# A cross network of six layers: x0 read in four-row runs, every x0 transpose on TensorE, the program order fixed

## The chip, the cores and the metric

The kernel runs on one core of a Trainium2 chip. The metric is the device time of one execution, in microseconds. The kernel before takes 142.92 us (median of three runs, 142.19 to 143.85).

## The reference

The input `x0` is a 4096 x 416 matrix in bfloat16, with six weight matrices of 416 x 416 and six bias rows of 416. Each layer multiplies the current `x` by a matrix, adds a bias row, multiplies the result element by element with `x0` and adds the old `x`:

```python
def reference(x0, ws, bs):
    x = x0
    for l in range(ws.shape[0]):
        x = x0 * (x @ ws[l] + bs[l]) + x
    return x
```

The rows of the batch never mix, so the kernel is free to choose which row lies in which place, if input and output agree.

## The kernel before, in words

The first five layers work on the transposed matrix: features on the 128 partitions, batch rows along the free dimension. The 416 features are three full blocks of 128 (`m` or `k` = 0, 1, 2; tile `XM`) and a remainder of 32 (tile `XR`, which stacks four column groups of 32 partitions each). The 4096 rows are two slabs of 2048 (`s` = 0, 1), and a slab is four groups `g` of 512 columns.

One **unit** is one layer on one slab; there are ten, and the first of them also prepares the data. On TensorE a unit runs 12 matmuls of 512 columns for `m` = 0 (three `k` for each group, line 167), four small matmuls with the remainder's weights (line 172) that finish block 0, four that open block 1, then 12 and 12 for blocks 1 and 2, the four that finish block 2, and the remainder's own product `pr` (lines 178 and 183). ScalarE then adds the bias while it moves each pair of groups out of PSUM into a tile `t` (line 154; line 160 for the remainder), and VectorE multiplies by `x0` and adds the old `x` (lines 155 and 156; 161 and 162).

The last layer works the other way around: rows on the partitions, features along the free dimension, so that its result can be written out as it is. Eight **quads** of four 128-row blocks each take 12 matmuls (line 258), four with the remainder (264) and four with the bias row (267). ScalarE copies out of PSUM (282), VectorE multiplies by `X0rows` (283) and adds the x of the layer before (284 for the 384 full features, 285 for the 32 of the remainder), and SyncE's queue (SP) starts the write (286). For this the x of the fifth layer has to be turned back: DMA transposes on SP write its three full blocks into `XLrows` (line 190) and its remainder into `scrR` (line 242). The last quad is handled in four single blocks (lines 289 to 293).

At the start, `x0` arrives in chunks of four 128-row blocks (`X0rows`, lines 81 to 85, with layer 0's weights behind the first chunk). TensorE transposes slab 0's chunks into PSUM, 12 transposes a chunk (line 125), and VectorE (127) and ScalarE (129) copy them to `XM[0]`; 16 small transposes make the remainder (136, 138). Slab 1 comes by another way: its blocks 0 and 1 through two DMA transposes straight from `x0` (line 96), its block 2 and remainder from a tile `slab1` by TensorE (lines 144, 136), in the middle of unit 0. Its plain rows, which only the last layer reads, are loaded later (102, 103).

All PSUM tiles come from one pool of four slots of 4 KB a partition. A pair of result tiles takes two slots; a group of transposes, `pr` or `tpr` takes one. A slot is free again when its reader has finished.

The order in which each engine runs its instructions is set, in the kernel before, by the framework's planner, which starts from the program's order and may move an instruction ahead of another one that is not ready by its reckoning. Each engine then works strictly in that order. SP takes its DMA issues in turn, and each carries one of eight semaphores, so an issue also waits until the eighth DMA before it has landed.

Of the kernel before, what the change touches and what calls it, by code (L numbers as in the profile page):

```python
# [16 lines left out]
def kernel(  # L17
# [27 lines left out]
    x0_v = x0.rearrange("(bt p) d -> p bt d", p=P)  # L45
    out_v = out.rearrange("(bt p) d -> p bt d", p=P)
# [13 lines left out]
    XLrows = big.tile([P, NBT, NK * P], BF16)  # L60
    scrR = [big.tile([P, 4, P], BF16, name=f"scrR{s}") for s in range(NS)]
    slab1 = big.tile([P, 16, 160], BF16)
# [13 lines left out]
    pe_filler(7)  # L76
# [4 lines left out]
    nc.sync.dma_start(X0rows[:, 0:4, :], x0_v[:, 0:4, :])  # L81
    load_wm(0)
    nc.sync.dma_start(X0rows[:, 4:8, :], x0_v[:, 4:8, :])
    nc.sync.dma_start(X0rows[:, 8:12, :], x0_v[:, 8:12, :])
    nc.sync.dma_start(X0rows[:, 12:16, :], x0_v[:, 12:16, :])
# [4 lines left out]
    with nc.allow_non_contiguous_dma(reason="tiny corner blocks"):  # L90
        for g in range(NG):
            nc.gpsimd.dma_start(WD[32 * g:32 * g + 32, :, g, :], ws[:, NK * P:D, NK * P:D].rearrange("l r n -> r l n"))  # L92
# [9 lines left out]
    nc.sync.dma_start(X0rows[:, 16:24, :], x0_v[:, 16:24, :])  # L102
    nc.sync.dma_start(X0rows[:, 24:32, :], x0_v[:, 24:32, :])
    for g in range(NG):
        nc.gpsimd.dma_start(bLr[32 * g:32 * g + 1, :], bs[LL:LL + 1, :])

# [12 lines left out]
    def x0_transposes_main(g):  # L119
        tp = psum.tile([P, NK, CW], BF16, tag="ps", name="tp")  # L120
        c0 = col0(0, g)
        for k in range(NK):
            for i in range(4):
                bt = 4 * g + i
                nc.tensor.transpose(tp[:, k, 128 * i:128 * i + 128], X0rows[:, bt, 128 * k:128 * k + 128], ident[:])  # L125
            if k < 2:
                nc.vector.tensor_copy(XM[0][:, k, c0:c0 + CW], tp[:, k, :])  # L127
            else:
                nc.scalar.copy(XM[0][:, k, c0:c0 + CW], tp[:, k, :])  # L129

    def x0_transposes_rem(s):
        tpr = psum.tile([P, CW], BF16, tag="ps", name="tpr")
        for i in range(4):
            for g in range(NG):
                src = X0rows[:, 4 * g + i, NK * P:D] if s == 0 else slab1[:, 4 * g + i, P:P + R]
                nc.tensor.transpose(tpr[32 * g:32 * g + 32, 128 * i:128 * i + 128], src, ident[:],
                                    tile_position=(0, 32 * g))
        nc.scalar.copy(XR[0][:, CW * s:CW * s + CW], tpr[:])

    def x0_transposes_k2_s1():  # L140
        for h in range(2):
            tk = psum.tile([P, 2 * CW], BF16, tag="ps", name="tk")
            for j in range(8):
                nc.tensor.transpose(tk[:, 128 * j:128 * j + 128], slab1[:, 8 * h + j, 0:P], ident[:])  # L144
            c0 = SW + 2 * CW * h
            if h == 0:
                nc.vector.tensor_copy(XM[0][:, 2, c0:c0 + 2 * CW], tk[:])
            else:
                nc.scalar.copy(XM[0][:, 2, c0:c0 + 2 * CW], tk[:])  # L149
# [14 lines left out]
    def mm_full(l, s, m, g, pts, cur, first, last):  # L164
        c0 = col0(s, g)
        for k in range(NK):
            nc.tensor.matmul(pts[g // 2][:, g % 2, :], lhsT=WM[:, l, k, 128 * m:128 * m + 128], rhs=cur[:, k, c0:c0 + CW],  # L167
                             start=(first and k == 0), stop=(last and k == NK - 1))
# [25 lines left out]
    for l in range(LL):  # L194
        nxt, nxtR = XM[1 + (l % 2)], XR[1 + (l % 2)]
        feeds_last = (l == LL - 1)
        for s in range(NS):
# [3 lines left out]
            if first_unit:  # L201
                x0_transposes_main(0)
                bias_setup()
                x0_transposes_main(1)
                mm_full(l, s, 0, 0, pts0, cur, True, False)
                x0_transposes_main(2)
                mm_full(l, s, 0, 1, pts0, cur, True, False)
                x0_transposes_main(3)
                mm_full(l, s, 0, 2, pts0, cur, True, False)
                x0_transposes_rem(0)  # L210
                mm_full(l, s, 0, 3, pts0, cur, True, False)
            else:
                for g in range(NG):
                    mm_full(l, s, 0, g, pts0, cur, True, False)
# [16 lines left out]
            if first_unit:  # L231
                x0_transposes_k2_s1()
                x0_transposes_rem(1)
            mm_row(l, s, 2, pts2, curR, False, True)
            pr = psum.tile([P, CW], FP32, tag="ps", name="pr")
            mm_rem(l, s, pr, cur, curR)
            for h in range(2):
                ew_main(l, s, 2, h, pts2[h], cur, nxt)
            ew_rem(l, s, pr, curR, nxtR)
            if feeds_last:  # L240
                xl_dmat(s, 2, nxt)
                nc.sync.dma_start_transpose(out=scrR[s][:], in_=nxtR[:, CW * s:CW * s + CW])
# [27 lines left out]
    def ew_q(q, py):  # L270
        s, i = quads[q]
        last_quad = (q == NQ - 1)
        for h in range(2):
            bts = [16 * s + 4 * (2 * h + gl) + i for gl in range(2)]
# [3 lines left out]
            x0v = X0rows[:, bts[0]:bts[1] + 1:4, :]  # L278
            xlv = XLrows[:, bts[0]:bts[1] + 1:4, :]
            xrv = scrR[s][:, i, 64 * h:64 * h + 64].rearrange("p (a r) -> p a r", a=2)  # L280
            if not last_quad:
                nc.scalar.copy(tv, py[h][:, :, 0:D])  # L282
                nc.vector.tensor_tensor(out=tv, in0=tv, in1=x0v, op=ALU.mult)  # L283
                nc.vector.tensor_tensor(out=o[:, :, 0:KD], in0=tv[:, :, 0:KD], in1=xlv, op=ALU.add)  # L284
                nc.vector.tensor_tensor(out=o[:, :, KD:D], in0=tv[:, :, KD:D], in1=xrv, op=ALU.add)
                nc.sync.dma_start(out_v[:, bts[0]:bts[1] + 1:4, :], o[:])
            else:
                for gl in range(2):
                    nc.scalar.copy(tv[:, gl, :], py[h][:, gl, 0:D])
                    nc.vector.tensor_tensor(out=tv[:, gl, :], in0=tv[:, gl, :], in1=X0rows[:, bts[gl], :], op=ALU.mult)  # L290
                    nc.vector.tensor_tensor(out=o[:, gl, 0:KD], in0=tv[:, gl, 0:KD], in1=XLrows[:, bts[gl], :], op=ALU.add)
                    nc.vector.tensor_tensor(out=o[:, gl, KD:D], in0=tv[:, gl, KD:D], in1=xrv[:, gl, :], op=ALU.add)
                    nc.sync.dma_start(out_v[:, bts[gl], :], o[:, gl, :])
# [40 lines left out]
```

## Time and profile before

| | |
|---|---|
| median of three runs | 142.92 us (142.19 to 143.85) |
| profiled execution, span from first to last instruction | 141.9 us |
| TensorE busy | 130.0 us, 92% of the span |
| VectorE busy | 109.3 us, 77% |
| ScalarE busy | 87.0 us, 61% |
| GpSimd busy | 8.4 us, 6% |
| chain that ended last | TensorE 71%, VectorE 11%, DMA 9%, ScalarE 3% |
| HBM read, written | 6.68 MB, 3.41 MB |

The profile is that of one execution. Its span runs from the first instruction to the last; the run's time also holds what lies around the span. Three stages have to be read apart: the start until unit 1 of ten begins on TensorE (about 26 us), the nine further units (to about 115 us), and the last layer with its writes.

### The profile page before, as it was taken

To read this page: it belongs to the slowest core of one execution; us is meant where nothing else is said; L and a number is where in the kernel's file an instruction comes from. 1 tells how busy PE (TensorE), PEld (TensorE's weight loads), DVE (VectorE), ACT (ScalarE), POOL (GpSimd) and SP (SyncE) were. 2 spreads that over 40 slices of the span, in tenths; PEclk is the share of its full clock that TensorE was granted. 3 is DMA by queue.
4 is the path that set the end of the run, shared out by engine and by line. 5 is a ranking of instruction groups with operands and counts; after the bars stand their busy time and mean duration, and the time that the engine had idled before them with its cause. 6 is when DMAs were issued, how large, how long until landed. Compare 5 with 4: busy or idle time off the path is not lost.

```text
span 141.9 us, 2405 instructions
## 1 busy us (share of the span) xinstructions
PE 130.0 (92%) x910; PEld 56.0 (39%) x910; DVE 109.3 (77%) x207; ACT 87.0 (61%) x97; POOL 8.4 (6%) x21
## 2 busy tenths in 40 slices
PE   5759998999999999999999999999999999999910
PEld 2426345434343343343333433433433345445400
DVE  1214178769878888898798799787987989999891
ACT  4011593875695695677657956956776578548530
POOL 8950000000000000000000000000000000000000
PEclk9968999999999999999999999999999999999995
DMA  4999999980000000000000000000089999965542
GB/s 136 294 280 130 232 249 273 330 251 10 0 2 0 0 7 0 0 0 0 0 5 0 0 0 0 5 0 0 0 166 173 146 200 187 229 226 178 175 162 92
DMA packets 31899, 14.69 MB, mean 104 GB/s; under 512 B 20618, under 2 KB 31888, under 8 KB 31888
## 3 DMA queue, kind: packets, MB, share of 16 engines
q1 hardware_dynamic: 31472, 14.38, 43.1%
q0 software_dynamic: 416, 0.16, 0.5%
q8 instruction: 7, 0.11, 0.3%
q14 instruction: 4, 0.03, 0.1%
HBM read 6.68 MB, written 3.41 MB: 71 GB/s over the span
## 4 chain that ended last, share of the span: by engine, by line
PE 71%; DVE 11%; DMA 9%; ACT 3%; issue 2%; SPq 1%; DVEq 0%
DMA X0rows<-in_x_dram 6%; PE pr L183 5%; DMA out_dram<-o 3%; PE pr L178 2%; DVE t L283 2%; DVE XM_87 L156 2%; DVE t L155 2%; DVE o L284 2%; ACT XM_86 L129 1%; PE pt_1184 L167 1%; PE pt_1166 L167 1%; PE pt_1081 L167 1%; PE pt_982 L167 1%; PE pt_784 L167 1%; PE pt_388 L167 1%
## 5 line engine op out<-in xcount | busy, mean ns | idle before, releaser
L167 PEld LDWEIGHTS <-WM 128*128 128x128 bf16 x360 | 33.7, 98 | 45.4 <-issue 8.6
L155 DVE TENSOR_TENSOR t<-t,XM_86 128x1024 bf16<-128x1024 bf16 x60 | 41.2, 686 | 13.5 <-ACT t L154 12.9
L156 DVE TENSOR_TENSOR XM_87<-t,XM_88 128x1024 bf16<-128x1024 bf16 x24 | 16.6, 690 | 2.1
L156 DVE TENSOR_TENSOR XM_88<-t,XM_87 128x1024 bf16<-128x1024 bf16 x24 | 16.6, 691 | 1.4
L258 PEld LDWEIGHTS <-XM_87 128*128 128x128 bf16 x96 | 9.0, 98 | 8.5 <-issue 1.8
L127 DVE COPY XM_86<-tp 128x512 bf16<-128x512 bf16 x8 | 3.3, 422 | 9.3 <-PE tp L125 9.3
L129 ACT COPY XM_86<-tp 128x512 bf16<-128x512 bf16 x4 | 2.3, 585 | 11.6 <-PE tp L125 11.6
L283 DVE TENSOR_TENSOR t<-t,X0rows 128x832 bf16<-128x832 bf16 x14 | 8.2, 586 | 0.9 <-ACT t L282 0.8
L156 DVE TENSOR_TENSOR XM_87<-t,XM_86 128x1024 bf16<-128x1024 bf16 x12 | 8.3, 690 | 0.3
L284 DVE TENSOR_TENSOR o<-t,XLrows 128x768 bf16<-128x768 bf16 x14 | 7.8, 557 | 0.5
L125 PE MATMUL tp<-ident,X0rows 128*128 128x128 bf16 x48 | 5.2, 250 | 2.9 <-DMA X0rows<-in_x_dram 1.7
L160 ACT ACTIVATE t<-pr,bR 128x512 bf16<-128x512 f32 x10 | 6.9, 689 | 0.0
L125 PEld LDWEIGHTS <-X0rows 128*128 128x128 bf16 x48 | 3.9, 114 | 5.5 <-DMA X0rows<-in_x_dram 2.8
L172 PEld LDWEIGHTS <-WR 32*128 32x128 bf16 x120 | 2.4, 91 | 8.4 <-issue 8.1
L74 PE MATMUL wps<-warm 128*128 128x512 bf16 x7 | 3.2, 630 | 1.5 <-DVE dz L67 1.5
L161 DVE TENSOR_TENSOR t<-t,XR_89 128x512 bf16<-128x512 bf16 x10 | 4.2, 418 | 0.0
L183 PEld LDWEIGHTS <-WM 128*32 128x32 bf16 x120 | 3.2, 97 | 2.2
L183 PE MATMUL pr<-XM_88,WM 128*32 128x512 bf16 x48 | 3.3, 379 | 0.0
L183 PE MATMUL pr<-XM_87,WM 128*32 128x512 bf16 x48 | 3.3, 379 | 0.0
L167 PE MATMUL pt_141<-XM_86,WM 128*128 128x512 bf16 x6 | 2.8, 544 | 0.1
L149 ACT COPY XM_86<-tk 128x1024 bf16<-128x1024 bf16 x1 | 1.0, 1012 | 2.3 <-PE tk L144 2.3
L92 POOL DMA_DIRECT2D WD<-in_ws_dram x4 | 2.3, 573 | 0.9 <-DMA WR<-in_ws_dram 0.9
(288 smaller groups left out, 255.4 us busy)
## 6 DMA issues: line engine op xcount, KB each, us to landing
out_dram<-o SPq DMA_DIRECT2D x14, 208.0 KB, 2.2
WM<-in_ws_dram SPq DMA_DIRECT2D x6, 312.0 KB, 6.0
X0rows<-in_x_dram SPq DMA_DIRECT2D x4, 416.0 KB, 7.5
X0rows<-in_x_dram SPq DMA_DIRECT2D x2, 832.0 KB, 8.8
slab_85<-in_x_dram SPq DMA_DIRECT2D x1, 640.0 KB, 10.9
WR<-in_ws_dram SPq DMA_DIRECT2D x4, 130.0 KB, 6.4
out_dram<-o SPq DMA_DIRECT2D x4, 104.0 KB, 1.7
WR<-in_ws_dram POOLq DMA_DIRECT2D x4, 26.0 KB, 5.7
```

What stands on the lines that cost most here:

```text
L125: nc.tensor.transpose(tp[:, k, 128 * i:128 * i + 128], X0rows[:, bt, 128 * k:128 * k + 128], ident[:])
L127: nc.vector.tensor_copy(XM[0][:, k, c0:c0 + CW], tp[:, k, :])
L129: nc.scalar.copy(XM[0][:, k, c0:c0 + CW], tp[:, k, :])
L155: nc.vector.tensor_tensor(out=t[:], in0=t[:], in1=XM[0][:, m, c0:c0 + 2 * CW], op=ALU.mult)
L156: nc.vector.tensor_tensor(out=nxt[:, m, c0:c0 + 2 * CW], in0=t[:], in1=cur[:, m, c0:c0 + 2 * CW], op=ALU.add)
L160: nc.scalar.activation(tr[:, 0:CW], pr[:], ACT.Identity, bias=bR[:, l:l + 1], scale=1.0)
L161: nc.vector.tensor_tensor(out=tr[:, 0:CW], in0=tr[:, 0:CW], in1=XR[0][:, CW * s:CW * s + CW], op=ALU.mult)
L167: nc.tensor.matmul(pts[g // 2][:, g % 2, :], lhsT=WM[:, l, k, 128 * m:128 * m + 128], rhs=cur[:, k, c0:c0 + CW], start=(first and k == 0), ...
L183: nc.tensor.matmul(pr[32 * g:32 * g + 32, :], lhsT=WM[:, l, k, NK * P:D], rhs=cur[:, k, c0:c0 + CW], start=False, stop=(k == NK - 1), tile ...
L258: nc.tensor.matmul(py[g // 2][:, g % 2, 0:D], lhsT=cur[:, k, q_cols(q, g)], rhs=WM[:, l, k, :], start=((not rem_first) and k == 0), stop=( ...
L283: nc.vector.tensor_tensor(out=tv, in0=tv, in1=x0v, op=ALU.mult)
L284: nc.vector.tensor_tensor(out=o[:, :, 0:KD], in0=tv[:, :, 0:KD], in1=xlv, op=ALU.add)
```

## The change

- **Row order.** Chunk `c` now holds rows 512c to 512c+511 with row 512c + 4p + j in partition p, place j. A partition's share of a chunk is four neighbouring rows, one run of 3328 bytes in place of four of 832. The output uses the same order, in writes of one row per partition and block as before.
- **Loads.** Chunk 0 is loaded in two halves of two rows each. The four chunks of slab 1 follow chunk 3 at once and are the only load of those rows; the tile `slab1`, the two DMA transposes from `x0` and the two later loads are gone. `WD`, the remainder's corner weights, is no longer loaded by DMA but copied by GpSimd out of `WR`.
- **Transposes of slab 1.** All three blocks are made by TensorE in unit 0, 16 transposes each, half of each copied by VectorE and half by ScalarE. Blocks 0 and 1 stand where block 2 stood; block 2 and the remainder stand behind `pr`, and ahead of the bias additions for block 2 of unit 0.
- **Slab 0's chunks.** The 12 transposes run block by block; two of the three 512-column results leave in one VectorE copy of 1024 columns. Of the seven warm-up matmuls, two move behind chunk 0's transposes. The bias transposes move behind the first matmuls.
- **Order.** `tc.manual_schedule()` fixes each engine's order to that of the program; the planner no longer moves anything.
- **Last layer.** The remainder of the fifth layer's result goes by four DMA transposes a slab (32 partitions each) straight into the last 32 columns of `XLrows`, in place of one a slab into `scrR`. The two additions (lines 284 and 285) become one of 832 columns.

```diff
-    x0_v = x0.rearrange("(bt p) d -> p bt d", p=P)
-    out_v = out.rearrange("(bt p) d -> p bt d", p=P)
+    x0_v = x0.rearrange("(c p j) d -> p c j d", p=P, j=4)
+    out_v = out.rearrange("(c p j) d -> p c j d", p=P, j=4)
...
+    ctx.enter_context(tc.manual_schedule())
...
-    pe_filler(7)
+    pe_filler(5)
...
+    load_x0(0, 0, 2)
+    load_x0(0, 2, 4)
     load_wm(0)
+    for c in range(1, 4):
+        load_x0(c)
...
-    with nc.allow_non_contiguous_dma(reason="320B row segments"):
-        nc.sync.dma_start(slab1[:], x0_v[:, 16:32, 2 * P:D])
-    for k in range(2):
-        nc.sync.dma_start_transpose(out=XM[0][:, k, SW:2 * SW], in_=x0[SW:2 * SW, 128 * k:128 * k + 128])
+    for c in range(4, 8):
+        load_x0(c)
...
+    for g in range(NG):
+        nc.gpsimd.tensor_copy(WD[32 * g:32 * g + 32, 0, g, :], WR[32 * g:32 * g + 32, 0, NK * P:D])
...
     def x0_transposes_main(g):
+        tg = psum.tile([P, 4 * CW], BF16, tag="ps", name="tg")
+        for i in range(4):
+            for k in range(NK):
+                c = CW * k + 128 * i
+                nc.tensor.transpose(tg[:, c:c + 128], X0rows[:, 4 * g + i, 128 * k:128 * k + 128], ident[:])
+        nc.vector.tensor_copy(XM[0][:, 0:2, c0:c0 + CW], tg[:, 0:2 * CW].rearrange("p (k c) -> p k c", k=2))
+        nc.scalar.copy(XM[0][:, 2, c0:c0 + CW], tg[:, 2 * CW:3 * CW])
...
+    def x0_transposes_s1(k):
+        tk = psum.tile([P, 2, 2 * CW], BF16, tag="ps", name="tk")
         for h in range(2):
             for j in range(8):
+                nc.tensor.transpose(tk[:, h, 128 * j:128 * j + 128], X0rows[:, 16 + 8 * h + j, 128 * k:128 * k + 128], ident[:])
             c0 = SW + 2 * CW * h
             if h == 0:
+                nc.vector.tensor_copy(XM[0][:, k, c0:c0 + 2 * CW], tk[:, h, :])
             else:
+                nc.scalar.copy(XM[0][:, k, c0:c0 + 2 * CW], tk[:, h, :])
...
             if first_unit:
                 x0_transposes_main(0)
-                bias_setup()
+                pe_filler(2)
                 x0_transposes_main(1)
                 mm_full(l, s, 0, 0, pts0, cur, True, False)
+                bias_setup()
...
             if first_unit:
-                x0_transposes_k2_s1()
-                x0_transposes_rem(1)
+                x0_transposes_s1(0)
+                x0_transposes_s1(1)
             mm_row(l, s, 2, pts2, curR, False, True)
             pr = psum.tile([P, CW], FP32, tag="ps", name="pr")
             mm_rem(l, s, pr, cur, curR)
+            if first_unit:
+                x0_transposes_s1(2)
+                x0_transposes_rem(1)
             for h in range(2):
                 ew_main(l, s, 2, h, pts2[h], cur, nxt)
             ew_rem(l, s, pr, curR, nxtR)
             if feeds_last:
                 xl_dmat(s, 2, nxt)
-                nc.sync.dma_start_transpose(out=scrR[s][:], in_=nxtR[:, CW * s:CW * s + CW])
+                for g in range(NG):
+                    nc.sync.dma_start_transpose(out=XLrows[:, 16 * s + 4 * g:16 * s + 4 * g + 4, NK * P:D],
+                                                in_=nxtR[32 * g:32 * g + 32, CW * s:CW * s + CW])
...
-                nc.vector.tensor_tensor(out=o[:, :, 0:KD], in0=tv[:, :, 0:KD], in1=xlv, op=ALU.add)
-                nc.vector.tensor_tensor(out=o[:, :, KD:D], in0=tv[:, :, KD:D], in1=xrv, op=ALU.add)
+                nc.vector.tensor_tensor(out=o[:], in0=tv, in1=XLrows[:, bts[0]:bts[1] + 1:4, :], op=ALU.add)
```

More of the change, by code (lines that the diff above doesn't have):

```diff
@@ L59 @@
     X0rows = big.tile([P, NBT, D], BF16)
-    XLrows = big.tile([P, NBT, NK * P], BF16)
-    scrR = [big.tile([P, 4, P], BF16, name=f"scrR{s}") for s in range(NS)]
-    slab1 = big.tile([P, 16, 160], BF16)
+    XLrows = big.tile([P, NBT, D], BF16)
     XM = [big.tile([P, NK, B], BF16, name=f"XM{i}") for i in range(3)]
     XR = [big.tile([P, NS * CW], BF16, name=f"XR{i}") for i in range(3)]
+    ctx.enter_context(tc.manual_schedule())
     nc.vector.memset(warm[:], 0.5)
@@ L165, in mm_full @@
         c0 = col0(s, g)
-        for k in range(NK):
+        ks = (0, 1, 2)
+        for n, k in enumerate(ks):
             nc.tensor.matmul(pts[g // 2][:, g % 2, :], lhsT=WM[:, l, k, 128 * m:128 * m + 128], rhs=cur[:, k, c0:c0 + CW],
-                             start=(first and k == 0), stop=(last and k == NK - 1))
+                             start=(first and n == 0), stop=(last and n == NK - 1))
     def mm_row(l, s, m, pts, curR, first, last):
@@ L241 @@
                 xl_dmat(s, 2, nxt)
[L242 removed]
+                for g in range(NG):
+                    nc.sync.dma_start_transpose(out=XLrows[:, 16 * s + 4 * g:16 * s + 4 * g + 4, NK * P:D],
+                                                in_=nxtR[32 * g:32 * g + 32, CW * s:CW * s + CW])
         cur, curR = nxt, nxtR
@@ L273, in ew_q @@
         for h in range(2):
-            bts = [16 * s + 4 * (2 * h + gl) + i for gl in range(2)]
+            c = 4 * s + 2 * h
+            bts = [4 * c + i, 4 * c + 4 + i]
             t = tpool.tile([P, 2 * CW], BF16, name="t")
```

42 lines of the change are left out of this document (9 added, 33 removed).

## The prediction

> **What bounds the kernel now.** I read the page first, then busy time by stage, then the chain of waits, then the start in order of time.
>
> ```profile
> span 141.9 us, 2405 instructions
> ...
> PEclk9968999999999999999999999999999999999995
> ```
>
> The stages (start:end, length, busy time of PE, PEld, DVE, ACT and POOL, granted clock, DMA share, GB/s):
>
> ```profile
> 5.00:8.40 3.40, 1.09 (x16) 0.70 (x14) 1.09 (x4) 0.58 (x1) 2.51 (x5) 1.00 1.03 308
> 8.40:11.90 3.50, 3.03 (x16) 1.76 (x16) 1.10 (x3) 0.00 (x0) 1.55 (x4) 0.51 1.22 232
> 26.10:114.60 88.50, 88.50 (x581) 35.22 (x578) 76.31 (x126) 61.27 (x64) 0.00 (x0) 1.00 0.20 42
> 119.70:124.90 5.20, 5.20 (x43) 2.62 (x41) 4.82 (x13) 3.26 (x5) 0.00 (x0) 1.00 0.98 240
> ```
>
> From 26.1 to 114.6 PE never rests: nine units of 9.83 us. A pair of quads of the last layer is full of PE too (5.20 of 5.20). The change touches no matmul of these, and a fixed order can't pack a full PE any better, so it can act only before 26.1 and in the tail. The chain (start, length, work) gives the start:
>
> ```profile
> 2.31 0.51 SPq L84
> ...
> 2.86 9.17 DMA X0rows<-in_x_dram
> ...
> 16.83 0.39 PE pt_141 L172 x2
> ...
> 24.46 0.41 PE tpr L136 x16
> ...
> 25.19 0.33 PE pr L178 x4
> 25.52 0.65 PE pr L183 x12
> 26.16 1.40 PE pt_370 L167 x6
> 27.57 1.29 PE pt_371 L167 x6
> ...
> 114.63 1.16 PE pt_1269 L258 x6
> ```
>
> Chunk 3 of x0 lands at 12.03. At 17.26, which I call T0, ScalarE begins unit 0's bias additions. Unit 1's first matmul is at 26.16, T0 + 8.9. So the change is worth (new T0) + (new distance from T0 to unit 1) - 26.16, and what the tail gives.
>
> **From T0 to unit 1: longer.** Unit 0 now, in order of time:
>
> ```profile
> 17.26 1.11 ACT L154 ACTIVATE t<-pt_141,bM 128x1024 bf16<-128x1024 f32 x1 [0.48 <-PE pt_142 L172]
> ...
> 18.27 1.11 ACT L154 ACTIVATE t<-pt_142,bM 128x1024 bf16<-128x1024 f32 x1
> 18.41 0.69 DVE L155 TENSOR_TENSOR t<-t,XM_86 128x1024 bf16<-128x1024 bf16 x1 [3.43 <-ACT t L154]
> ...
> 22.57 1.06 PE L144 MATMUL tk<-ident,slab_85 128*128 128x128 bf16 x16
> ...
> 23.66 1.01 ACT L149 COPY XM_86<-tk 128x1024 bf16<-128x1024 bf16 x1 [2.27 <-PE tk L144]
> 23.73 0.68 DVE L147 COPY XM_86<-tk 128x1024 bf16<-128x1024 bf16 x1
> ...
> 25.58 0.59 ACT L138 COPY XR_89<-tpr 128x512 bf16<-128x512 bf16 x1
> ```
>
> I lay the new order on these prices, relative to T0. The first 16 transposes start as before at 22.57 - 17.26 = 5.31 and end at 6.37; block 1's end at 7.43. VectorE is busy with eight products and sums from 18.41 to 23.73 in both kernels, so its copies run 6.47 to 7.15 and to 7.83; ScalarE's run 6.40 to 7.41 and to 8.46. The four L172 matmuls (16.83 to 17.26: 0.43) end at 7.86, `pr` (0.33 + 0.65) at 8.84, block 2's transposes at 9.90. Now comes the new wait. The four PSUM slots hold the two result tiles of block 2, `pr` and block 2's transposes. The first three are read by bias additions that stand, in the fixed order, behind the copy of the remainder, so that remainder's slot can only be the transposes' own: it waits for ScalarE's half (9.92 + 1.01 = 10.93). Then 0.41 of transposes and a ScalarE copy of 0.59 end at 12.0, which frees the first slot for unit 1. Its second slot comes 1.11 later, before PE has done the 1.29 of the first pair. So unit 1 starts at T0 + 12.0, not + 8.9: 3.1 us lost, of which 2.12 are 32 transposes that DMA did before and most of the rest is PE waiting for slots. Unit 1's own bias additions come later than unit 0's last, so nothing further runs on.
>
> **T0: earlier.** The start, and two answers on DMA packets (from 1.5 to 9.15 us, then from 2.5 to 4.0):
>
> ```profile
> 4.10 0.10 PEld L125 LDWEIGHTS <-X0rows 128*128 128x128 bf16 x1 [0.38 <-DMA X0rows<-in_x_dram]
> ...
> 6.94 0.18 PE L115 MATMUL pb<-ident,bsb 6*32 6x6 bf16 x4
> ...
> 8.86 0.34 PEld L125 LDWEIGHTS <-X0rows 128*128 128x128 bf16 x4 [1.83 <-DMA X0rows<-in_x_dram]
> ```
>
> ```profile
> DMA packets 2970, 2.18 MB, mean 285 GB/s; under 512 B 557, under 2 KB 2970, under 8 KB 2970
> ```
>
> ```profile
> DMA packets 639, 0.52 MB, mean 346 GB/s; under 512 B 16, under 2 KB 639, under 8 KB 639
> ```
>
> By 9.15 us 2.18 MB had moved, more than the 2.02 MB of four chunks (0.426 each) and layer 0's weights (0.319). Yet chunk 1 was there only at 8.86 and chunk 3 at 12.03: 557 packets of the slab behind had passed already, so the chunks wait for the slowest of the 16 DMA engines. The late end for the new kernel is therefore as now: 8.86 and 12.03. The early end has no laggard and the 346 GB/s of the second row throughout: chunk 0 (1.23 us at that rate) was used at 4.10, an offset of 2.87; chunk 1 closes 1.17 MB, 2.87 + 3.38 = 6.25; chunk 3 closes 2.02 MB, 8.72. Long runs cut the packets of a chunk from 512 to 128 or 256, so a delay per packet shrinks; what makes an engine lag the trace doesn't say. I take the middle: 7.55 and 10.4. The extra issue ahead of chunk 3 (0.51 on SP) hides behind engines that are still moving chunk 0.
>
> Here the Trainium skill speaks against the change: "DMA: Bandwidth & Descriptors", Specifications, has 512 bytes as enough for line rate, and runs of 832 are above it. By it nothing lands sooner, which is the slow rival below; the laggard here can't be explained by it.
>
> Behind chunk 1 PE has three groups of 12 transposes (1.06 x 12/16 = 0.80 each), four of three matmuls (half of 1.29, 0.65 each), seven bias transposes (0.18 x 7/4 = 0.32), the remainder (0.41) and the L172 matmuls (0.43): 6.16 us; behind chunk 3, 0.80 + 0.65 + 0.41 + 0.65 + 0.43 = 2.94. The copies out of PSUM, one of 1024 columns for two of 512 among them, run beside the next matmuls. What happens to chunk 0 (two halves, five warm-up matmuls and two later) ends before chunk 1 is there and costs nothing; if chunk 1 came at once, it would be some 0.43 us (two of the 1.29 for six). T0 is the later of 7.55 + 6.16 = 13.7 and 10.4 + 2.94 = 13.3, at full clock: 13.7, against 17.26.
>
> Slab 1's four chunks are needed at T0 + 5.3 = 19.0. 1.70 MB at 285 GB/s behind 10.4 is 16.4: covered by 2.6 us. `WD` is needed by `pr` at T0 + 7.9 = 21.6; its source lands about 10:
>
> ```profile
> WR<-in_ws_dram POOLq DMA_DIRECT2D x4, 26.0 KB, 5.7
> ```
>
> No row prices GpSimd's copies, but 11 us of cover take them; at worst they would delay `pr` by what exceeds it.
>
> **The last layer: a little shorter.**
>
> ```profile
> 119.46 0.58 DVE L283 TENSOR_TENSOR t<-t,X0rows 128x832 bf16<-128x832 bf16 x1
> ...
> 120.08 0.56 DVE L284 TENSOR_TENSOR o<-t,XLrows 128x768 bf16<-128x768 bf16 x1
> ...
> 120.56 0.18 DVE L285 TENSOR_TENSOR o<-t,scrR_83 128x64 bf16<-128x64 bf16 x1
> 120.66 0.58 DVE L283 TENSOR_TENSOR t<-t,X0rows 128x832 bf16<-128x832 bf16 x1
> ...
> 129.15 0.56 DVE L284 TENSOR_TENSOR o<-t,XLrows 128x768 bf16<-128x768 bf16 x1
> ...
> 133.67 0.59 DVE L283 TENSOR_TENSOR t<-t,X0rows 128x832 bf16<-128x832 bf16 x1 [0.27 <-ACT t L282]
> ```
>
> Half a quad takes 0.62 + 0.48 + 0.10 = 1.20 on DVE; one addition of 832 columns takes 0.48 x 832/768 = 0.52 for 0.58, saving 0.06. That counts only where DVE is the bound, behind the last wait at 133.67: four halves, 0.24 us. Ahead of that it is slack.
>
> SP gets eight issues for two:
>
> ```profile
> 110.16 1.56 SPq L242 DMA_TRANSPOSE scrR_83<-XR_90  x1
> ...
> 120.15 1.39 SPq L242 DMA_TRANSPOSE scrR_84<-XR_90  x1
> 121.63 14.92 SPq L286 DMA_DIRECT2D out_dram<-o  x14
> ```
>
> ```profile
> L190 SPq DMA_TRANSPOSE XLrows<-XM_87 x6: 1698/1912/2964, 102.1 to 117.9; - x6
> ```
>
> ```profile
> scrR_83<-XR_90 SPq DMA_TRANSPOSE x1, 4.3
> scrR_84<-XR_90 SPq DMA_TRANSPOSE x1, 2.6
> ```
>
> Each new one moves a quarter: 0.35 to 1.56 on SP; I take 1.4, since L190 with four times the data takes only 1.9. In the times of before: four from 110.16 to 115.8, three L190 (held back by them) to 121.5, the last of slab 1's begins at 125.7 and lands 2.6 later at 128.3. DVE reads it at 129.15: 0.85 to spare. Writes start 5.4 us later, queued behind them on SP, and catch up: an issue about every half microsecond against a tile every 1.14.
>
> **Sum.** 13.7 + 12.0 - 26.16 - 0.24 = -0.7 against the span of 141.9. The median of 142.92 lies 1.0 above that span, and I keep that distance: 142.2.
>
> **Rivals.**
> - *No laggard.* Long runs take the lag away, chunk 1 at 6.25: T0 = 12.4, 2.0 us faster, 140.9. For it: packets of a chunk fall to a quarter. Against: no row ties the lag to packets. Chance 0.24.
> - *The join doesn't wait.* If the slots or the order don't work as I read them, the 1.03 behind 9.90 and the 0.7 until 12.0 go: 1.7 less, 140.5. Chance 0.08.
> - *Half clock.* From 8.40 PE ran at 0.51 after a stretch with 1.09 of 3.40 busy. If that returns in this window, 3.5 us of the work behind chunk 1 run at half speed: T0 = 15.4, +1.0, 143.9. New is an earlier chunk 1 and two fillers in the stretch, which make about 1.8 of 3.4 busy. Chance 0.13. The Trainium skill ("TensorE: Matmul & The Clock Gate", Part 1) has the clock halve after an idle window; by that rule it stays full, but the trace halved it behind a window that was a third busy.
> - *Nothing lands sooner (slower).* Chunk 1 at 8.86 makes T0 15.0, and with half clock until 11.9 (as now) 16.5: +2.1, 145.0. It decides from chunk 1 later than 8.2, where T0 passes 14.4 and the gain no longer pays the 3.1 at the join. For it: DMA is full already at 346 GB/s. Chance 0.15.
> - *SP's transposes bind.* At 1.56 each and 4.3 to land, the last is there at 131.1, 2.0 late; DVE's slack (5.20 - 4 x 1.14 = 0.6 a pair) leaves 1.4: 143.6. Chance 0.07.
>
> My forecast keeps 0.33; a fifth of it lies beyond 1% faster.
>
> **Numbers.** One per cent, 1.4 us, is what a measurement of this kernel can tell from no change. Faster: 0.24 + 0.08 + 0.07 = 0.39. Slower: 0.15, and 0.05 from the upper ends of half clock and SP: 0.20. Same: 0.41. The likeliest case alone spans 141.2 to 143.2; the range reaches to the fast rivals' side, 140.1, and into the slow one, 144.3.
>
> **What would show it.** Chunk 1's first use between 6.3 and 8.9; the ScalarE start near 13.7; the remainder's transposes idling for the ScalarE copy of block 2; unit 1 about 12 behind T0; units of 9.83; an addition of 832 columns at about 0.6; no DVE wait at the second slab's first quad. A distance T0 to unit 1 near 10, or unit 1 before 24, would make me wrong.

## The result and the profile after

The changed kernel is slower: 150.2 us (median of four, 149.18 to 150.96) against 143.38 for the kernel before beside it (142.19 to 144.44), a ratio of 1.052 (95% interval 1.045 to 1.059). The forecast was 142.2, with 144.3 as its upper end. Where a ratio stands beside a median in what follows, it leaves out disturbed executions, so the two need not divide out.

The profiled execution of the changed kernel is the 149.18. Its page begins:

```profile
span 147.4 us, 2458 instructions
...
PEclk9968999999999999999999999999999999999975
```

The span is 5.4 us longer than before's 141.9. The view by stages (start:end, length, busy time of PE, PEld, DVE, ACT and POOL, granted clock, DMA share, GB/s) says where it isn't:

```profile
5.35:8.76 3.41, 1.48 (x17) 0.88 (x15) 0.69 (x2) 0.59 (x1) 0.40 (x2) 1.00 1.01 351
8.76:12.17 3.41, 3.41 (x25) 2.06 (x24) 1.37 (x4) 0.99 (x2) 2.29 (x6) 0.50 1.03 399
25.80:29.20 3.40, 1.77 (x28) 1.13 (x21) 0.69 (x1) 1.17 (x2) 0.00 (x0) 1.00 0.00 0
30.54:119.00 88.46, 88.46 (x577) 35.17 (x576) 78.15 (x126) 62.18 (x64) 0.00 (x0) 1.00 0.12 20
```

The nine units are what they were: 88.46 us, all of it PE work. But PE was half idle in a stretch ahead of them (1.77 of 3.40), and from 8.76 to 12.17 it ran at half clock again. The start in order of time, then the join:

```profile
7.62 0.84 PE L125 MATMUL tg<-ident,X0rows 128*128 128x128 bf16 x12 [1.93 <-DMA X0rows<-in_x_dram]
...
15.28 1.11 ACT L152 ACTIVATE t<-pt,bM 128x1024 bf16<-128x1024 f32 x1 [0.48 <-PE pt L171]
...
20.58 0.61 PE L142 MATMUL tk<-ident,X0rows 128*128 128x128 bf16 x8
...
21.93 0.68 DVE L145 COPY XM<-tk 128x1024 bf16<-128x1024 bf16 x1
22.66 1.05 PE L142 MATMUL tk<-ident,X0rows 128*128 128x128 bf16 x16 [1.47 <-DVE XM L145]
...
23.31 1.01 ACT L147 COPY XM<-tk 128x1024 bf16<-128x1024 bf16 x1 [3.90 <-PE tk L142]
...
24.50 0.61 PE L142 MATMUL tk<-ident,X0rows 128*128 128x128 bf16 x8 [0.78 <-DVE XM L145]
...
26.34 0.62 PE L142 MATMUL tk<-ident,X0rows 128*128 128x128 bf16 x8
27.00 0.69 DVE L145 COPY XM<-tk 128x1024 bf16<-128x1024 bf16 x1 [2.56 <-PE tk L142]
27.75 0.61 PE L142 MATMUL tk<-ident,X0rows 128*128 128x128 bf16 x8 [0.78 <-DVE XM L145]
...
28.39 1.01 ACT L147 COPY XM<-tk 128x1024 bf16<-128x1024 bf16 x1 [2.23 <-PE tk L142]
29.45 0.41 PE L133 MATMUL tpr<-ident,X0rows 128*32 128x128 bf16 x16 [1.10 <-ACT XM L147]
...
30.54 0.81 PE L166 MATMUL pt<-XM,WM 128*128 128x512 bf16 x3 [0.68 <-ACT XR L136]
```

T0, ScalarE's first bias addition, is at 15.28 (before 17.26): 2.0 us won. Unit 1 begins at 30.54, 15.3 behind T0 (before 8.8). A block's 16 transposes don't run as one: PE makes eight, waits for VectorE's copy of them, and only then makes the other eight, which go into another part of the same PSUM tile (waits of 1.47, 0.78 and 0.78, 3.0 together).

The end, first SP's queue, then two rows of VectorE, then the landing times (the last column, median us from issue to landing):

```profile
115.03 5.08 SPq L246 DMA_TRANSPOSE XLrows<-XR  x4
...
127.76 5.54 SPq L246 DMA_TRANSPOSE XLrows<-XR  x4
133.41 8.36 SPq L288 DMA_DIRECT2D out_dram<-o  x14
141.86 2.16 SPq L294 DMA_DIRECT2D out_dram<-o  x4
```

```profile
128.44 0.59 DVE L287 TENSOR_TENSOR o<-t,XLrows 128x832 bf16<-128x832 bf16 x1
...
142.86 0.38 DVE L293 TENSOR_TENSOR o<-t,XLrows 128x416 bf16<-128x416 bf16 x1
```

```profile
out_dram<-o SPq DMA_DIRECT2D x14, 208.0 KB, 3.1
...
out_dram<-o SPq DMA_DIRECT2D x4, 104.0 KB, 2.6
```

VectorE doesn't wait for the transposes, but the first write leaves at 133.41 (before 121.63), fourteen go out within 8.36 us (before 14.92), and the last ones are down 2.6 us after their issue. In the kernel before the same two rows were:

```profile
out_dram<-o SPq DMA_DIRECT2D x14, 208.0 KB, 2.2
...
out_dram<-o SPq DMA_DIRECT2D x4, 104.0 KB, 1.7
```

So from VectorE's end to the end of the span it is 4.1 us for 3.0. The account of the 5.4 us between the two profiles: T0 -2.0, the join +6.4, nine units 0, from unit 10's end to VectorE's end -0.2, behind that +1.1. The medians lie 6.8 apart; the profile is the fastest of the changed kernel's executions, and what the others lost besides isn't in a profile of this kernel.

### The profile page after: what moved, and what is told of

The parts are those of the page before. It is cut to its first block, busy times and chain, and to the rows that moved or that the text cites. A ratio compares the mean times of both kernels' runs of the same rounds, so it can differ in the third digit from the quotient of the medians.

```text
span 147.4 us, 2458 instructions
## 1 busy us (share of the span) xinstructions
PE 131.4 (89%) x942; PEld 58.0 (39%) x942; DVE 111.0 (75%) x187; ACT 89.2 (61%) x99; POOL 9.0 (6%) x25
## 3 DMA queue, kind: packets, MB, share of 16 engines
HBM read 5.97 MB, written 3.41 MB: 64 GB/s over the span
## 4 chain that ended last, share of the span: by engine, by line
PE 79%; DVE 8%; DMA 4%; ACT 3%; issue 2%; SPq 1%; ACTq 0%
PE pt L166 50%; PE pt L263 10%; PE pt L171 6%; PE pr L182 4%; DMA X0rows<-in_x_dram 4%; PE pr L177 2%; PE tg L125 2%; PE tk L142 2%; DVE XM L154 2%; DVE t L153 2%; DVE XM L145 1%; PE pt L269 1%; DVE t L292 1%; PE pt L272 1%; DVE o L293 1%
## 5 line engine op out<-in xcount | busy, mean ns | idle before, releaser
L166 PE MATMUL pt<-XM,WM 128*128 128x512 bf16 x360 | 82.6, 382 | 0.7 <-ACT XR L136 0.7
L152 ACT ACTIVATE t<-pt,bM 128x1024 bf16<-128x1024 f32 x60 | 62.5, 1114 | 26.8 <-PE pt L171 26.8
L153 DVE TENSOR_TENSOR t<-t,XM 128x1024 bf16<-128x1024 bf16 x60 | 41.4, 690 | 11.5 <-ACT t L152 10.6
L154 DVE TENSOR_TENSOR XM<-t,XM 128x1024 bf16<-128x1024 bf16 x60 | 41.5, 692 | 4.6
L263 PE MATMUL pt<-WM,XM 128*128 128x416 bf16 x96 | 17.7, 340 | 0.0
L285 ACT CAST t<-pt 128x832 bf16<-128x832 f32 x14 | 11.3, 855 | 6.7 <-PE pt L272 6.1
L263 PEld LDWEIGHTS <-XM 128*128 128x128 bf16 x96 | 9.0, 98 | 8.5 <-issue 1.8
L171 PE MATMUL pt<-XR,WR 32*128 32x512 bf16 x120 | 10.0, 381 | 0.1
L287 DVE TENSOR_TENSOR o<-t,XLrows 128x832 bf16<-128x832 bf16 x14 | 8.3, 592 | 0.5
L182 PE MATMUL pr<-XM,WM 128*32 128x512 bf16 x120 | 8.2, 379 | 0.0
```

The lines of the kernel that those rows point to most:

```text
L152: nc.scalar.activation(t[:], pt[:].rearrange("p a b -> p (a b)"), ACT.Identity, bias=bM[:, m, l:l + 1], scale=1.0)
L153: nc.vector.tensor_tensor(out=t[:], in0=t[:], in1=XM[0][:, m, c0:c0 + 2 * CW], op=ALU.mult)
L154: nc.vector.tensor_tensor(out=nxt[:, m, c0:c0 + 2 * CW], in0=t[:], in1=cur[:, m, c0:c0 + 2 * CW], op=ALU.add)
L171: nc.tensor.matmul(pts[g // 2][:, g % 2, :], lhsT=WR[32 * g:32 * g + 32, l, 128 * m:128 * m + 128], rhs=curR[32 * g:32 * g + 32, CW * s:CW ...
L182: nc.tensor.matmul(pr[32 * g:32 * g + 32, :], lhsT=WM[:, l, k, NK * P:D], rhs=cur[:, k, c0:c0 + CW], start=False, stop=(k == NK - 1), tile ...
L263: nc.tensor.matmul(py[g // 2][:, g % 2, 0:D], lhsT=cur[:, k, q_cols(q, g)], rhs=WM[:, l, k, :], start=((not rem_first) and k == 0), stop=( ...
```

## The experiments

The kernel before, run beside them, had medians of 143.95 (third to sixth row of the table), 144.22 (next four) and 143.25 (last four). The table holds the marks of each profile in us: first transposes of chunk 1, T0, T0 to unit 1, unit 1's length, from VectorE's end to the span's end, and the stretches at half clock from some 5 us on to 40. Unit 1 begins here with the first matmul of line 167 (in before's numbering) behind unit 0's `pr`. Two of the forecasts below name distances of 14.62 and 9.6, going by the kernels copies last and order only, in which it is 13.39 and 8.93: they rest on a count of matmuls, and some traces lack a matmul record here and there.

| kernel | chunk 1 | T0 | T0 to unit 1 | unit 1 | end | half clock | median |
|---|---|---|---|---|---|---|---|
| before | 8.87 | 17.26 | 8.84 | 9.83 | 2.98 | 8.43-11.84 | 143.38 |
| after | 7.62 | 15.28 | 15.27 | 9.82 | 4.12 | 8.76-12.17 | 150.20 |
| order only, on before | 7.78 | 21.79 | 8.93 | 9.83 | 2.83 | 9.05-22.70 | 148.49 |
| planner free | 7.88 | 15.32 | 11.02 | 10.52 | 4.46 | to 10.68 | 146.04 |
| copies last | 8.25 | 15.69 | 13.39 | 11.11 | 4.69 | 7.84-11.26, 28.32-31.74 | 149.93 |
| one remainder transpose | 7.54 | 15.10 | 16.79 | 11.18 | 2.83 | to 10.80, 24.45-27.86, 31.28-34.69 | 149.37 |
| single rows | 7.77 | 13.94 | 15.09 | 11.50 | 3.64 | 29.08-32.49 | 150.48 |
| more fillers | 7.68 | 13.86 | 16.90 | 11.24 | 4.42 | 23.43-26.85, 30.26-33.67 | 150.45 |
| bias first | 7.67 | 15.33 | 11.37 | 15.35 | 4.78 | 8.46-11.88, 28.94-35.77 | 151.74 |
| two tiles | 7.95 | 15.38 | 13.96 | 9.82 | 4.53 | to 10.72 | 150.47 |
| two blocks by DMA | 8.20 | 15.82 | 10.91 | 9.82 | 4.96 | 8.18-11.59 | 147.74 |
| before, grouped | 8.33 | 14.68 | 8.84 | 9.83 | 2.98 | none behind 7.42 | 140.74 |
| the same, fixed order | 8.97 | 15.88 | 8.85 | 9.83 | 2.83 | none behind 7.13 | 141.31 |
| after, mended | 8.48 | 14.65 | 11.49 | 9.82 | 2.98 | none behind 6.76 | 143.09 |

**The fixed order alone, on the kernel of before.**

```diff
+    ctx.enter_context(tc.manual_schedule())
```

> The kernel before with its order fixed to the program's and nothing else changed. Theory (the order alone is harmless; the loss is made by what stands in it): the stage from ScalarE's first bias addition (T0) to unit 1's first matmul grows from 8.9 to at most 10.5 us, units stay at 9.83, time within 1.5 us of before. Rival (a fixed order by itself costs most of the loss): 4 us or more above before.

148.49 us, ratio 1.037 (1.027 to 1.047). The join is 8.9, as in before, so the order by itself doesn't make it long. But T0 is at 21.79, 4.5 us late, so the theory's time fails and the rival's holds, by another way than the join. This kernel in order of time, then by stages:

```profile
12.40 0.59 PE L127 MATMUL tp<-ident,X0rows 128*128 128x128 bf16 x4 [0.52 <-DVE XM L129]
13.50 0.59 PE L127 MATMUL tp<-ident,X0rows 128*128 128x128 bf16 x4 [0.52 <-DVE XM L129]
```

```profile
9.05:12.47 3.42, 2.39 (x14) 1.38 (x13) 0.85 (x2) 0.58 (x1) 0.61 (x2) 0.50 1.49 217
12.47:15.88 3.41, 2.58 (x14) 1.64 (x15) 0.48 (x2) 0.58 (x1) 0.00 (x0) 0.50 0.98 198
```

PE makes four transposes of a chunk, waits 0.52 for VectorE's copy of them (again one tile, different parts), and goes on; the planner had filled these waits with other groups' matmuls. With them PE is busy for 70 to 76% of a stretch at half clock, and the clock stays down for 13.65 us. The kernel of before, in order of time, has such a wait too:

```profile
6.47 0.38 PE L125 MATMUL tp<-ident,X0rows 128*128 128x128 bf16 x4 [0.52 <-DVE XM_86 L127]
```

**The planner given back to the changed kernel.**

```diff
-    ctx.enter_context(tc.manual_schedule())
```

> The changed kernel with the planner free to move instructions again. Theory (wait of the second half of a PSUM tile's transposes for the copy of its first half, which no order removes): T0 to unit 1 stays at 13 us or more, against 15.3 with the fixed order; at most 2.5 us faster than the changed kernel. Rival (the fixed order puts block 2's bias additions behind the copies and that is the loss): T0 to unit 1 falls to about 10 to 11, some 4 to 5 us faster than the changed kernel.

146.04 us, ratio 1.016 (1.001 to 1.030): some 4 us of the change's 7 go. The join falls to 11.0, the rival's figure, because the planner puts block 2's bias additions (on ScalarE) ahead of the last copies. It also lets unit 1 begin ahead of block 2's last eight transposes, so unit 1 takes 10.5, and at its end 3.5 us are won. T0 and the late end stay. This kernel in order of time:

```profile
22.04 1.11 ACT L151 ACTIVATE t<-pt,bM 128x1024 bf16<-128x1024 f32 x1 [2.60 <-PE pt L170]
...
25.16 1.13 ACT L151 ACTIVATE t<-pt,bM 128x1024 bf16<-128x1024 f32 x1
...
26.34 0.38 PE L165 MATMUL pt<-XM,WM 128*128 128x512 bf16 x1
...
26.81 0.61 PE L141 MATMUL tk<-ident,X0rows 128*128 128x128 bf16 x8
```

**Each block's copies behind all of its transposes.**

```diff
         for h in range(2):
             for j in range(8):
                 nc.tensor.transpose(tk[:, h, 128 * j:128 * j + 128], ...)
+        for h in range(2):
             c0 = SW + 2 * CW * h
```

> The changed kernel, but each block of slab 1 has its 16 transposes first and its two copies behind them, so that no transpose follows a copy out of the same tile. Theory (the three waits of 1.5, 0.8 and 0.8 us of PE for VectorE's copy of the first half go): T0 to unit 1 falls from 15.3 to about 13, 2 us faster than the changed kernel; the ScalarE copy may still start only when VectorE's has ended. Rival (PE waits for VectorE being busy and for slots, whatever the order of transposes): T0 to unit 1 stays at 15, time as the changed kernel's.

149.93 us, join 13.4. The theory's distance of about 13 is met, and the waits within a block go (32 transposes run without a break). But 1.9 us is not all 3.0 of the waits: some come back one step on, on ScalarE's copies, which queue behind VectorE's of the same tile. The time hardly moves, because in this profile unit 1 starts at half clock and takes 11.1: at its end 0.6 us is left. PE in this kernel, in order of time:

```profile
21.00 1.95 PE L142 MATMUL tk<-ident,X0rows 128*128 128x128 bf16 x32
...
24.12 0.40 PE L178 MATMUL pr<-XR,WD 128*32 128x512 bf16 x4 [0.84 <-ACT XM L148]
...
27.99 0.41 PE L133 MATMUL tpr<-ident,X0rows 128*32 128x128 bf16 x16 [1.82 <-ACT XM L148]
```

**The last layer's remainder as before.**

```diff
-                for g in range(NG):
-                    nc.sync.dma_start_transpose(out=XLrows[:, 16 * s + 4 * g:16 * s + 4 * g + 4, NK * P:D],
-                                                in_=nxtR[32 * g:32 * g + 32, CW * s:CW * s + CW])
+                nc.sync.dma_start_transpose(out=scrR[s][:], in_=nxtR[:, CW * s:CW * s + CW])
...
-                nc.vector.tensor_tensor(out=o[:], in0=tv, in1=XLrows[:, bts[0]:bts[1] + 1:4, :], op=ALU.add)
+                nc.vector.tensor_tensor(out=o[:, :, 0:KD], in0=tv[:, :, 0:KD], in1=XLrows[:, bts[0]:bts[1] + 1:4, :], op=ALU.add)
+                nc.vector.tensor_tensor(out=o[:, :, KD:D], in0=tv[:, :, KD:D], in1=xrv, op=ALU.add)
...
```

> The changed kernel with the last layer's remainder as before: one DMA transpose a slab and two additions. Theory (eight transposes on SP hold the writes back to 133.4, and the writes then queue up to the end): the first write starts 5 us or more earlier, the last one lands sooner, 1.0 to 1.5 us faster than the changed kernel. Rival (writes of rows that stand four apart in DRAM are slow by themselves): the last write still takes 2.6 us to land; within 0.5 us of the changed kernel.

149.37 us, ratio 1.041 (1.029 to 1.054). The end is back at 2.8 us although the rows are still written four apart, so it is the backlog on SP and not the place of the rows: theory held, rival fallen. SP's queue in this kernel:

```profile
117.80 1.26 SPq L246 DMA_TRANSPOSE scrR<-XR  x1
...
126.67 1.90 SPq L246 DMA_TRANSPOSE scrR<-XR  x1
128.66 15.04 SPq L289 DMA_DIRECT2D out_dram<-o  x14
```

One transpose of a whole remainder costs SP 1.26 and 1.90 (in before 1.56 and 1.39); a quarter of it, in the changed kernel, 1.27 and 1.39 (5.08 and 5.54 for four). The gain doesn't show clear of the scatter in the time: this profile has two stretches at half clock around the join (16.8 long), where the changed kernel's has none.

**The x0 rows one by one.**

```diff
-    x0_v = x0.rearrange("(c p j) d -> p c j d", p=P, j=4)
-    out_v = out.rearrange("(c p j) d -> p c j d", p=P, j=4)
+    x0_v = x0.rearrange("(c j p) d -> p c j d", p=P, j=4)
+    out_v = out.rearrange("(c j p) d -> p c j d", p=P, j=4)
```

> The changed kernel with the loads and the writes back in single rows of 832 bytes (a chunk's row p of block j is 128 j + p again); order and number of the loads stay. Theory of the prediction (long runs bring chunk 1 sooner): the thirteenth x0 transpose is back near 8.9 us, at least beyond 8.2, T0 at 16 or later, and the time at least 0.7 us above the changed kernel's 150.2. Rival A (the order of the loads does it: chunk 0 in halves, nothing of the slab behind ahead of chunks 1 to 3; the kernel of before in a fixed order had chunk 1 at 7.78 with short runs): chunk 1 within 0.4 of 7.62, T0 within 0.5 of 15.28, the time within 1 us of 150.2. Rival B for the end (rows written 4 apart are what lands late): from VectorE's last instruction to the end of the span back from 4.12 to 3.0 us.

Chunk 1 is used at 7.77, and at 8.20 in the other kernel with single rows (two blocks by DMA): the length of the runs buys nothing that shows. With before's loads it was used at 7.78, 8.33, 8.87 and 8.97, with the change's long runs at 7.54 to 8.48 in eight profiles: the loads' order may win some tenths, inside a spread of a microsecond. The theory falls; rival A holds on chunk 1. The time (147.85 to 152.47) is too scattered for a verdict. The end, 3.6 us, lies between rival B's 3.0 and the changed kernel's 4.1; it is 5.0 in the other kernel with single rows, and the experiment before brought it to 2.8 without them, so rival B falls too. T0 was 13.94, because here the clock stayed full. By stages:

```profile
5.18:8.60 3.42, 1.51 (x19) 0.97 (x17) 0.69 (x1) 0.59 (x1) 0.40 (x2) 1.00 1.06 331
8.60:12.01 3.41, 3.41 (x41) 2.17 (x38) 1.98 (x5) 1.17 (x2) 2.30 (x6) 1.00 1.11 333
```

**More warm-up matmuls behind chunk 0.**

```diff
-                pe_filler(2)
+                pe_filler(8)
```

> The changed kernel with eight warm-up matmuls for two behind chunk 0's transposes. Theory (the half clock from 8.76 to 12.17 follows a window of 3.4 us in which PE was under half busy, and costs T0 about half of 3.4 us): the clock is full from about 5.3 on, T0 at 13.7 (13.3 to 14.1) for 15.28, and the time falls by 1 to 1.8 us from 150.2, all of it ahead of T0; the distance from T0 to unit 1 stays within 0.5 of 15.3. Rival (T0 is set by chunk 3's landing or by the copies, not by the clock): T0 stays above 14.8.

T0 13.86: the forecast's 13.7, once the clock is full. The time is the same, 150.45: what T0 wins, the join loses at half clock. By stages, with this kernel:

```profile
20.02:23.43 3.41, 1.29 (x21) 1.17 (x21) 1.97 (x3) 1.01 (x1) 0.00 (x0) 1.00 0.23 69
23.43:26.85 3.42, 3.42 (x33) 1.42 (x31) 0.00 (x0) 1.01 (x1) 0.00 (x0) 0.50 0.00 0
26.85:30.26 3.41, 1.33 (x29) 1.05 (x28) 0.69 (x1) 1.16 (x2) 0.00 (x0) 1.00 0.00 0
```

The waits of the join leave PE 1.29 us busy of 3.41, and the next stretch runs at 0.50. The theory was right on T0 and wrong on the time.

**Block 2's bias additions ahead of the last transposes' copies.** (The copies stand last in their blocks here as well.)

```diff
-            if first_unit:
-                x0_transposes_s1(2)
-                x0_transposes_rem(1)
             for h in range(2):
                 ew_main(l, s, 2, h, pts2[h], cur, nxt)
             ew_rem(l, s, pr, curR, nxtR)
+            if first_unit:
+                x0_transposes_s1(2)
+                x0_transposes_rem(1)
```

> The changed kernel with each block's 16 transposes ahead of its two copies, and the last block's transposes and the remainder moved behind block 2's bias additions, products and sums in the fixed order. Theory (the join is long because the slots of block 2 are read by bias additions that queue on ScalarE behind the copies, and the copies behind each other): the distance from T0 to unit 1 falls from 15.27 to 10.5 to 12, and the time by 3 to 4.5 us, to about 146. Rival (PE's own work there, 24 transposes more per half than before, sets the distance, or the waits only change places as they did when the copies alone were moved, 14.62): at least 13.5, and the time above 148.5.

The distance is 11.4 as expected, but the time rises to 151.74, because unit 1 now stops inside itself. PE and VectorE in order of time:

```profile
26.71 0.59 PE L167 MATMUL pt<-XM,WM 128*128 128x512 bf16 x2 [0.55 <-ACT t L153]
...
29.14 0.68 DVE L146 COPY XM<-tk 128x1024 bf16<-128x1024 bf16 x1
...
29.88 1.44 PE L167 MATMUL pt<-XM,WM 128*128 128x512 bf16 x3 [2.58 <-DVE XM L146]
```

Its third matmul needs block 2 of slab 1, whose copy now stands behind all of unit 0's products and sums on VectorE. Half clock follows, and unit 1 takes 15.35. So the join has to be measured to the end of unit 1.

**One PSUM tile for each half block.**

```diff
-        tk = psum.tile([P, 2, 2 * CW], BF16, tag="ps", name="tk")
         for h in range(2):
+            tk = psum.tile([P, 2 * CW], BF16, tag="ps", name="tk")
...
```

> The changed kernel with one PSUM tile for each half of a block of the slab behind (eight transposes and one copy each) in place of one tile of both halves; nothing else moves. Theory (the wait goes by tile: a transpose waits for a copy out of another part of the same tile, and so does a copy for another copy): the three waits of PE on VectorE's copy of the same block (1.47, 0.78, 0.78 in the changed kernel) are gone, and ScalarE's copy no longer starts behind VectorE's; the distance falls from 15.27 to 12.5 to 14 and the time by 1 to 2.5 us; waits for slots appear in their place, which is why it isn't more. Rival (the waits are for the slot or for VectorE's queue, whatever the tile): distance within 0.7 of 15.27, time within 1 us of 150.2.

This kernel's join in order of time:

```profile
20.68 1.06 PE L142 MATMUL tk<-ident,X0rows 128*128 128x128 bf16 x16
...
21.78 1.01 ACT L147 COPY XM<-tk 128x1024 bf16<-128x1024 bf16 x1 [2.27 <-PE tk L142]
22.03 0.68 DVE L145 COPY XM<-tk 128x1024 bf16<-128x1024 bf16 x1
22.76 1.05 PE L142 MATMUL tk<-ident,X0rows 128*128 128x128 bf16 x16 [1.02 <-DVE XM L145]
```

The halves of blocks 0 and 1 now run together and ScalarE's copy starts ahead of VectorE's: the wait went by tile. The distance is 14.0, inside the expected 12.5 to 14; the rest goes to waits for slots, since each half now takes one of the four. The median doesn't show it (148.45 to 151.86); the ratio is 1.036 (1.024 to 1.048) for the changed kernel's 1.052.

**Blocks 0 and 1 of slab 1 by DMA again.** (With single rows.)

```diff
-                x0_transposes_s1(0)
-                x0_transposes_s1(1)
...
+    for k in range(2):
+        nc.sync.dma_start_transpose(out=XM[0][:, k, SW:2 * SW], in_=x0[SW:2 * SW, 128 * k:128 * k + 128])
```

> The changed kernel with its x0 loads and writes in single rows, and blocks 0 and 1 of the slab behind transposed by two DMA transposes again, as before the change; block 2, the remainder, the fixed order and the last layer stay as changed. Theory (the join is long because of the 32 transposes and four copies that TensorE, VectorE and ScalarE took over, with their waits): the distance from T0 to unit 1 is 10.8 or less, for 15.27 in the changed kernel and 15.09 with single rows alone, unit 1 takes 9.9, and the time is 145 to 147. Rival (the fixed order by itself makes it long): 12.5 or more, the time above 148.

147.74 us, ratio 1.015 (1.006 to 1.025), join 10.9 for 15.1: 4.2 of the 6.4 us come with the 32 transposes and their copies. It is just above the 10.8 expected and well below the rival's 12.5, which falls; block 2's two waits (0.78 and 1.10 in this profile too) and its late place are the rest.

**Before, with only its start regrouped.** `x0_transposes_main` is the change's; the planner, the loads and all behind T0 are before's.

```diff
...
                 x0_transposes_main(0)
-                bias_setup()
+                pe_filler(8)
                 x0_transposes_main(1)
                 mm_full(l, s, 0, 0, pts0, cur, True, False)
+                bias_setup()
```

> The kernel of before, loads, DMA transposes, planner and last layer untouched, with two edits ahead of T0: the twelve transposes of a chunk stand together ahead of their two copies, as in the change, and eight warm-up matmuls follow chunk 0's twelve (the bias transposes come behind the first three matmuls). Theory (T0 is 17.3 in before because of the waits within a chunk and the half clock from 8.43 to 11.84, not because x0 lands late): chunk 1 used at 7.7 to 8.9, the clock full from about 5.5 on, T0 at 13.8 to 15.0, the distance to unit 1 within 0.8 of 8.84, and the time 2 to 3.5 us below the kernel of before, at 140 to 142. Rival (T0 hangs on the loads, which only the change moves): T0 above 16 and the time within 1 us of before.

140.74 us, ratio 0.982 (0.978 to 0.987): 1.8% below the kernel before, clear of the scatter; the rival falls. By stages:

```profile
4.01:7.42 3.41, 3.41 (x19) 2.00 (x18) 0.69 (x1) 0.58 (x1) 3.00 (x6) 1.00 0.97 276
7.42:10.83 3.41, 3.41 (x40) 2.19 (x39) 0.94 (x3) 0.58 (x1) 2.06 (x4) 1.00 1.21 273
21.07:24.48 3.41, 2.84 (x40) 1.25 (x40) 2.06 (x4) 3.40 (x5) 0.00 (x0) 1.00 1.10 292
```

The clock is full from 7.42 at the latest (the trace has no record of the clock ahead of that, so the 1.00 in the first row says nothing), T0 is at 14.68 with the old loads, and the join is 8.8 as in before.

**The same with the fixed order.**

```diff
+    ctx.enter_context(tc.manual_schedule())
```

> The same two edits to the kernel of before, and the fixed program order besides. Theory (a fixed order costs little by itself where no engine waits inside a chunk's transposes: with the order alone fixed the time was 148.49, nearly all of it from T0 at 21.79): T0 within 0.5 of the same kernel with the planner, the distance to unit 1 at 9.6, the time within 1.5 us of it and below before. Rival (the fixed order costs some 4 us wherever it stands): the time at 144 or above.

141.31 us, ratio 0.988 (0.982 to 0.994), join 8.9. T0 is 1.2 later than with the planner, not 0.5: chunks 1 and 3 were used later in this profile (8.97 and 12.72 for 8.33 and 11.52). The fixed order costs nothing that can be told where no group waits within itself.

**The changed kernel mended.** Planner, two tiles, eight warm-up matmuls and the old remainder (the edits above) together; long runs and all transposes on TensorE stay.

> The changed kernel with what the earlier runs point to: the planner in place of the fixed order, one PSUM tile for each half block, eight warm-up matmuls behind chunk 0, and the last layer's remainder as before (one transpose for a slab). Runs of four rows and all x0 transposes on TensorE stay. Theory (all of the loss lies in the half clock, the join and the backlog of SP): T0 at 13.9, distance 11.5 to 12.4, from VectorE's last instruction to the end 3.0, the time 142 to 144.5, no more than 1% from the kernel of before. Rival (32 transposes more on TensorE cost more than that, in windows of half clock behind unit 0): above 146.

143.09 us, ratio 1.000 (0.997 to 1.003); the rival falls. These four edits give back all that the change lost against before. T0 is 14.65 for the 13.9 expected (chunk 1 was used at 8.48), and what is won there (2.6 us) the join takes back (11.5 for 8.8); the 32 transposes more on TensorE take 2.1 of it as TensorE's own work.

## Why the prediction was wrong

- **The bound, right.** Nine units of 9.83 us, no idle PE, untouched by the order: 88.46 us after as before.
- **Chunk 1 and T0's other terms, right; the reason, wrong.** Chunk 1 was forecast at 7.55 and used at 7.62, but not for its long runs: single rows give 7.77. That it came so close is partly luck: 7.55 was the middle of two bounds, and the same loads were used at up to 8.48 in other profiles. The rival in which nothing lands sooner falls on the number. The Trainium skill ("DMA: Bandwidth & Descriptors", Specifications) holds runs of 512 bytes to be enough for line rate; single rows of 832 bytes, used as early as runs of 3328, agree.
- **T0 = 7.55 + 6.16 = 13.7 "at full clock", wrong by 1.6.** Measured 15.28; the half-clock rival had 15.4, at a chance of 0.13. Its estimate that the two fillers would make PE 1.8 of 3.4 busy was too high (1.48), and the profile of before had shown what a third-busy stretch does. With eight fillers T0 was 13.86: the term is right, the clock assumed was wrong.
- **The join, T0 + 12.0, wrong by 3.3: the step that failed.** It took each block's 16 transposes as one run of 1.06, held up by slots alone. The transposes start where it said (20.58 for 20.59), but one half waits for the copy of the other because both lie in one tile: the three waits (1.47, 0.78, 0.78) make 3.0 of the 3.3. So `pr` ends 2.2 late and the remainder's transposes start 3.2 late (29.45 for T0 + 10.93 = 26.21). The wait for the remainder's slot itself came as forecast (1.10 for ScalarE's copy of block 2). Two tiles per block take 1.3 us off, as slots then hold the transposes up; two blocks by DMA take 4.2 off and the planner 4.2, of which 3.5 are left at the end of unit 1. A row of before's own trace had shown such a wait and was not used: the one at 6.47 above, the third part of a tile that waits 0.52 for the copy of the second.
- **"Unit 1's own bias additions come later", right for this kernel, but idle PE has a second price** that the forecast set at nothing: where the join leaves PE busy for little of a stretch (1.29 and 1.33 of 3.41 in the kernel with more fillers), the next 3.4 us run at half clock (there twice, distance 16.9).
- **The last layer.** VectorE's saving (-0.24) came as -0.15, an addition of 832 columns took 0.59, about the 0.6 expected, and SP's transposes 1.27 to 1.39 for 1.4, without a wait on VectorE: that rival falls. "Writes start 5.4 us later ... and catch up" is where 1.1 us went: SP caught up, but the fourteen writes then went out in 8.4 us, and the last four took 2.6 us to land for 1.7. With the old remainder the end was 2.8 again.
- **The distance from span to time.** The forecast kept 1.0 us. The profile after has 1.8 (149.18 for 147.4), so the profile of before was probably that of its slowest execution (143.85); this touches both kernels alike.

The result lies 8 us above the forecast: 1.6 from the clock, 3.3 from the join, 1.2 from the end, and some 2 between the profile and the medians. That the fixed order could lose what the planner did wasn't among the rivals; the planner free gave 4 us back.

## What to carry to other kernels

Before laying out a stretch by hand, look in the trace for waits between parts of one tile: in these kernels a producer that fills a tile in pieces waits for each piece's reader. Other work between the pieces hides that wait, and a tile per piece removes it only as far as slots are free. Cost an idle stretch of TensorE twice, for itself and for the half clock that may follow, and judge an edit at the start only at the first mark behind which nothing varies (here the end of unit 1). Small transfers issued ahead of the output on the same queue cost a place in the queue each, and the writes that bunch up behind them are paid for at the end.

## What the runs showed of the hardware

- **The clock follows fixed stretches of 3.41 us.** Over all fourteen profiles, each stretch of the first 40 us at full clock in which PE was busy for less than 43% was followed by one at half clock (ten of them, 24 to 42.7%), and none with 56% or more was. Those between went both ways: 43% in the changed kernel (1.48 of 3.41), 46% and 51% in two others were halved; 44% with single rows (1.51 of 3.42) and 51% in the changed kernel's join (1.74 of 3.41) were not. At half clock, shares of 70 to 76% kept it there in the kernel with only the order fixed, for 13.65 us, and 73% did with the bias additions first; 73 and 76% released it with the copies last and with one remainder transpose. The stretches begin at another moment in each profile (5.02, 5.35, 5.18, 6.37), so the same start ran at half clock from 8.76 to 12.17 in the changed kernel and up to 10.72 with two tiles. The Trainium skill ("TensorE: Matmul & The Clock Gate", Part 1) has free-running windows of this length, which agrees, and half clock after an idle window; here 43% busy was idle enough.
- **A DMA transpose costs SP's queue nearly as much for a quarter of the data**: 1.27 and 1.39 us in the changed kernel, against 1.26 and 1.90 for a whole remainder (one remainder transpose) and 1.56 and 1.39 in the kernel before.
